# Second weights by neighbouring rows, first weights by every fourth column, in a recurrence followed by a gated MLP

## The chip, the cores and the metric

The kernel runs on one core of one Trainium2 chip. The metric is the time of one execution on the device, in microseconds. The core has five engines that run their own instruction streams: PE (TensorE: matrix products), DVE (VectorE), ACT (ScalarE), POOL (GpSimd) and SP (SyncE, which here only issues transfers). PEld stands for the loads of PE's stationary operand, which are instructions of their own. Transfers are carried by 16 DMA engines that all issuing queues share.

## The reference

The inputs are `q`, `k`, `v` and `alpha` of shape batch 4, heads 8, steps 768, head size 48, and two weight matrices. A recurrence runs over the steps of each head, and its outputs, 3072 tokens of 384 numbers, go through an MLP whose activation is `h * cos(h)`.

```python
for t in range(S):                                   # S = 768
    state = alpha[:, :, t, :, None] * state + np.einsum('bhd,bhe->bhde', k[:, :, t], v[:, :, t])
    y[:, :, t] = np.einsum('bhd,bhde->bhe', q[:, :, t], state)
...
x = y.transpose(0, 2, 1, 3).reshape(B * S, H * D)    # 3072 x 384
h = x @ w_in                                         # w_in: 384 x 2048
g = h * np.cos(h)
return g @ w_out                                     # w_out: 2048 x 384
```

The order in which the 2048 hidden columns are numbered does not matter to the result, as long as a column of `w_in` and the row of `w_out` with the same number meet in the second product.

## The kernel before

The work is cut into 12 blocks J of 256 tokens (three to a batch entry). For each block the recurrence is computed in chunks: logarithms of alpha and their running sums (`ln`, `cums0`, `cums`), exponentials (`icp`, `exps`), scaled keys and queries (`scale_k`, `scale_q`), transposes (`trans`), scores and mask, the states (`outer`, `add_state`, `decay_state`), and the transposed output (`yT`), which is evicted to `xT[J]` with 384 rows in three groups of 128 partitions and 256 token columns. Both `cums0` and `cums` end with small products in line 182: a load of 128x128 stationary numbers and a matrix product with 2 moving columns.

The MLP follows for the same block. `mlp1(J, u)` (line 390) makes one of four groups u of 512 hidden columns: `FW` = 4 tiles of 128 columns, each of `KT` = 3 accumulated products, 12 in all, with a 128x128 piece of `w1` as the stationary operand and 256 columns of `xT` as the moving one. `cosine` (ACT, line 396) and `gate` (DVE, line 401) turn the four tiles into `gsb[J]`. `mlp2` (line 419) multiplies with 16 tiles of `w2`: there `gsb` is the stationary operand and the 384 columns of `w2` move. Over the kernel there are 576 products of line 390.

Both weight matrices lie in SBUF for the whole run, in bfloat16; DRAM holds them in float32. `w1` is `[128, 3, 2048]`: partition p of group kk holds row 128 kk + p of `w_in`. `w2` is `[128, 16, 384]`. Each comes in four transfers of 384 KB (as written) that POOL issues, `load_w1(u)` (line 126) and `load_w2(u)` (line 132). They convert on the way and travel in POOL's own DMA queue, one after the other. The inputs of a block (`load`, line 110) are issued by SP, with runs of 384 bytes.

The order of the instructions on each engine is written out by hand: `PLAN` gives every step of every block a number, and the steps are emitted in that order. Where a transfer depends on nothing it is sent early; only the load of `a` for block 2 waits, until the products of `yT(1)` are done (`GATES`), and what SP issues after it stands behind it. Products of zeros (`idle`, line 445) fill some gaps of PE at the start.

Of the kernel before, what the change touches and what calls it, by code (L numbers as in the profile page):

```python
# [16 lines left out]
def kernel(  # L17
# [10 lines left out]
    nc = tc.nc  # L28
    B, H, S, D = q.shape
    DM, DF = moe_w_in.shape  # L30
    C = 128
# [8 lines left out]
    FW = 4  # L40
# [53 lines left out]
    w1 = consts.tile([C, KT, DF], BF, tag="w1", name="w1")  # L94
# [3 lines left out]
    xT, gsb = {}, {}  # L98
# [24 lines left out]
    WQ = FW * C  # L123
# [7 lines left out]
    def load_w2(u):  # L131
        nc.gpsimd.dma_start(
            out=w2[:, FW * u : FW * (u + 1)],
            in_=moe_w_out[u * WQ : (u + 1) * WQ, :].rearrange("(a p) d -> p a d", p=C),
        )

    act_now = [None]
# [245 lines left out]
    h_ps, c_sb, o_ps, o_sb = {}, {}, {}, {}  # L383

    def mlp1(J, u):
        h_ps[J, u] = ps.tile([C, FW, T2], FP, tag="h", name="h_ps", bufs=3)
        for f in range(FW):
            ft = u * FW + f
            for kk in range(KT):
                nc.tensor.matmul(h_ps[J, u][:, f, :], w1[:, kk, ft * C : (ft + 1) * C], xT[J][:, kk, :],  # L390
                                 start=(kk == 0), stop=(kk == KT - 1))

    def cosine(J, u):
# [47 lines left out]
    def idle(n):  # L441
# [6 lines left out]
    mults = {"DVE": nc.vector, "POOL": nc.gpsimd}  # L448
    steps = {
        "load": lambda J, nm: load(nm, J), "w1": load_w1, "w2": load_w2,  # L450
        "mula": mul_a, "ln": ln, "cums0": cums0, "cums": cums, "sub": sub, "icp": icp, "exps": exps, "eb": session,
        "sk": lambda J, e, eng="POOL": scale_k(J, e, mults[eng]), "sq": lambda J, e, eng="POOL": scale_q(J, e, mults[eng]),
        "castv": cast_v, "vst": stack_v, "vpe": stack_v_pe,
        "vev": lambda J, eng="DVE": evict_vs(J, copies[eng]), "decay": decay, "trans": trans,
        "evT": lambda J, c, eng="DVE": evict_T(J, c, copies[eng]), "scores": scores, "mask": mask, "outer": outer,
        "add": add_state, "state": decay_state, "yT": yT, "evy": lambda J, c, eng="ACT": evict_y(J, c, copies[eng]),
        "m1": mlp1, "sin": cosine, "gate": gate, "m2": mlp2, "evo": lambda J, c, eng="ACT": evict_o(J, c, copies[eng]),
        "out": store, "idle": idle,
    }
# [114 lines left out]
```

## Time and profile before

| | |
|---|---|
| time, median of 3 runs | 186.45 us (185.67 to 188.55) |
| the profiled execution | 185.78 us, span 184.0 us |
| granted TensorE clock | 0.999 |
| PE busy | 173.0 us, 94% of the span |
| PEld / DVE / ACT / POOL busy | 68% / 73% / 68% / 45% |
| moved by DMA | 29.47 MB in 60137 packets |

The span runs from the first instruction to the last; the execution takes 1.78 us more than that. Busy time of an engine is the time that its recorded instructions cover. The records of matrix products overlap, since a product starts before the one ahead of it has left the array, so a mean duration (273 ns in line 390) is not the time that one costs: that is the distance from one start to the next.

### The profile page before, as it was taken

The numbers are of one execution on the slowest core, as the hardware profiler recorded it, in microseconds if no ns is written. First come the engines' busy times: TensorE is split into PE (matmuls) and PEld (weight loads), VectorE is DVE, ScalarE is ACT, GpSimd is POOL, SyncE is SP. The second block draws the span as 40 slices with busy tenths as digits, with TensorE's granted clock in tenths as the row PEclk, the third lists the DMA queues.
The fourth block names the chain that finished last, engine by engine and source line by source line (L and its number), as shares of the span: only waits on it lengthen the run. The fifth ranks groups of instructions, "written<-read, shape, count | busy, mean of one in ns | idle before, by whom it ended". The sixth has DMA issues, their size and how long they took to land.

```text
span 184.0 us, 5742 instructions
## 1 busy us (share of the span) xinstructions
PE 173.0 (94%) x2457; PEld 125.5 (68%) x2458; DVE 134.5 (73%) x182; ACT 124.9 (68%) x157; POOL 83.5 (45%) x116
## 2 busy tenths in 40 slices
PE   7989579979999999999999999999899999999993
PEld 2445458646687776876787777876687677776672
DVE  7069777669999899799969898879587674734520
ACT  3745457789879999895978989869774517435201
POOL 5388550079883484939686093903901110000000
PEclk9999999999999999999999999999999999999999
DMA  6999999999999979963996579003420121010312
GB/s 146 261 248 224 216 202 206 262 256 257 261 213 262 304 170 278 260 164 85 278 289 154 140 215 245 18 6 88 143 71 4 41 88 51 0 43 4 127 44 86
DMA packets 60137, 29.47 MB, mean 160 GB/s; under 512 B 51024, under 2 KB 60112, under 8 KB 60112
## 3 DMA queue, kind: packets, MB, share of 16 engines
q1 hardware_dynamic: 56256, 25.86, 57.9%
q0 software_dynamic: 3712, 3.15, 10.6%
q8 instruction: 19, 0.31, 0.8%
q10 hardware_dynamic: 144, 0.10, 0.2%
q14 instruction: 6, 0.05, 0.1%
HBM read 25.17 MB, written 4.72 MB: 162 GB/s over the span
## 4 chain that ended last, share of the span: by engine, by line
PE 68%; DMA 11%; issue 7%; SPq 6%; POOL 5%; ACT 1%; DVE 1%; POOLq 0%; DVEq 0%
PE h_ps L390 28%; PE o_ps L419 26%; DMA v<-in_v_dram 6%; SPq L110 4%; PE y_ps L370 4%; DMA k<-in_k_dram 4%; PE A_ps L303 2%; PE T_ps L288 2%; PE U_ps L321 2%; SPq L246 2%; PE o_last L419 1%; DMA vs<-vp 1%; POOL un L343 1%; POOL a L154 1%; PE cums L168 1%
## 5 line engine op out<-in xcount | busy, mean ns | idle before, releaser
L401 DVE TENSOR_TENSOR gsb<-h_ps,c_sb 128x1024 bf16<-128x1024 f32 x48 | 58.4, 1222 | 20.0 <-ACT c_sb L396 18.8
L396 ACT ACTIVATE c_sb<-h_ps,halfpi 128x1024 bf16<-128x1024 f32 x48 | 53.4, 1114 | 28.5 <-PE h_ps L390 28.4
L390 PE MATMUL h_ps<-xT,w 128*128 128x256 bf16 x576 | 67.5, 273 | 0.7 <-DMA w<-in_moe_w_in_dram 0.5
L419 PE MATMUL o_ps<-w,gsb 128*128 128x384 bf16 x368 | 66.7, 326 | 0.0
L390 PEld LDWEIGHTS <-w 128*128 128x128 bf16 x576 | 55.4, 98 | 9.7 <-DMA w<-in_moe_w_in_dram 0.8
L419 PEld LDWEIGHTS <-gsb 128*128 128x128 bf16 x400 | 37.0, 98 | 20.8
L343 POOL TENSOR_TENSOR un<-us,c 128x384 bf16<-128x384 f32 x20 | 16.7, 836 | 33.1 <-DVE us L335 26.0
L309 DVE TENSOR_TENSOR A_sb<-A_ps,msk 128x1024 bf16<-128x1024 f32 x24 | 29.1, 1220 | 3.6 <-PE A_ps L303 3.4
L233 POOL TENSOR_TENSOR kh<-k,icp 128x384 bf16<-128x384 f32 x19 | 19.5, 1032 | 10.2 <-ACT lna L146 5.3
L237 POOL TENSOR_TENSOR qh<-q,cp 128x384 bf16<-128x384 f32 x19 | 18.8, 999 | 6.1 <-ACT cp L219 4.2
L154 POOL TENSOR_TENSOR a<-a 128x384 f32<-128x384 f32 x9 | 9.0, 997 | 11.8 <-DMA a<-in_alpha_dram 11.8
L240 POOL CAST vp<-v 128x768 bf16<-128x768 f32 x12 | 10.1, 853 | 6.4 <-DMA v<-in_v_dram 6.0
L146 ACT ACTIVATE lna<-a 128x768 bf16<-128x768 f32 x12 | 10.1, 842 | 4.1 <-DMA a<-in_alpha_dram 2.4
L141 ACT ACT_TABLE_LOAD x9 | 11.5, 1283 | 0.9 <-PEq L558 0.7
L294 DVE COPY qkT<-T_ps 128x1024 bf16<-128x1024 bf16 x17 | 11.4, 682 | 0.8 <-PE T_ps L288 0.8
L396 ACT ACT_TABLE_LOAD x9 | 11.5, 1283 | 0.2
L431 ACT COPY o_sb<-o_ps 128x384 f32<-128x384 f32 x10 | 4.8, 478 | 9.6 <-PE o_ps L419 9.6
L431 DVE COPY o_sb<-o_ps 128x384 f32<-128x384 f32 x13 | 7.2, 554 | 4.3 <-PE o_ps L419 4.2
L445 PE MATMUL idle_ps<-zeros 128*128 128x512 bf16 x28 | 9.0, 469 | 1.2 <-DVE halfpi L77 1.2
L379 DVE CAST xT<-y_ps 128x384 bf16<-128x384 f32 x14 | 7.7, 584 | 3.1 <-PE y_ps L370 2.9
L335 DVE TENSOR_TENSOR us<-U_ps,un 128x384 f32<-128x384 f32 x16 | 8.8, 551 | 1.3 <-PE U_ps L321 1.2
L303 PE MATMUL A_ps<-qkT 48*128 48x128 bf16 x192 | 8.7, 217 | 0.6 <-DVE qkT L294 0.5
(68 smaller groups left out, 149.2 us busy)
## 6 DMA issues: line engine op xcount, KB each, us to landing
a<-in_alpha_dram SPq DMA_DIRECT2D x12, 384.0 KB, 6.0
v<-in_v_dram SPq DMA_DIRECT2D x12, 384.0 KB, 6.1
k<-in_k_dram SPq DMA_DIRECT2D x12, 384.0 KB, 6.0
q<-in_q_dram SPq DMA_DIRECT2D x12, 384.0 KB, 6.2
out_dram<-o_sb SPq DMA_DIRECT2D x23, 192.0 KB, 2.3
vs<-vp SPq DMA_DIRECT2D x36, 64.0 KB, 2.8
w<-in_moe_w_in_dram POOLq DMA_DIRECT2D x4, 384.0 KB, 8.7
w<-in_moe_w_out_dram POOLq DMA_DIRECT2D x4, 384.0 KB, 10.7
```

The costliest lines, as they stand in the source:

```text
L141: nc.scalar.preload_act_table_set("natural_log_exp_and_others")
L233: eng.tensor_tensor(out=kh_t[J % NQ][:, e, :, 0:D], in0=kqv["k", J][:, :, e], in1=icp_, op=ALU.mult)
L237: eng.tensor_tensor(out=qh_t[J % NQ][:, e, :, 0:D], in0=kqv["q", J][:, :, e], in1=cp, op=ALU.mult)
L294: ins = copy(out=qkT_sb[J][:, c], in_=T_ps[J][:, c].rearrange("r n e s -> r n (e s)"))
L303: last = nc.tensor.matmul(A_ps[J, c][:, a, p, :], qkT[r, c, NP + p, :], qkT[r, c, p, :], start=True, stop=True)
L309: nc.vector.tensor_tensor(out=A_sb[J][:, c].rearrange("s a p t -> s (a p) t"), in0=A_ps.pop((J, c)).rearrange("s a p t -> s (a p) t"), in1 ...
L343: nc.gpsimd.tensor_tensor(out=u, in0=U_sum.pop(n), in1=c2_sb[J][:, :, c].unsqueeze(3).to_broadcast([C, NP, 2, D]), op=ALU.mult)
L390: nc.tensor.matmul(h_ps[J, u][:, f, :], w1[:, kk, ft * C : (ft + 1) * C], xT[J][:, kk, :], start=(kk == 0), stop=(kk == KT - 1))
L396: nc.scalar.activation(out=c_sb[J, u], in_=h_ps[J, u], func=AF.Sin, bias=halfpi, scale=1.0)
L401: nc.vector.tensor_tensor(out=gsb[J][:, u * FW : (u + 1) * FW], in0=h_ps.pop((J, u)), in1=c_sb.pop((J, u)), op=ALU.mult)
L419: nc.tensor.matmul(o[:, 0 : cols.stop - cols.start], gsb[J][:, ft, c * C : (c + 1) * C], w2[:, ft, cols], start=(done == 1 and ft == fts[0 ...
L431: copy(out=t, in_=o_ps.pop((J, c))[0][:, 0:DM])
```

## The change

Row f of the 512 rows of a transfer of `w_out` used to go to partition f mod 128, tile f div 128. Now it goes to partition f div 4, tile f mod 4: four neighbouring rows, 4 x 1536 bytes in DRAM, come to one partition, where they lie one behind the other. The transfer's shape goes from 128x4x384 to 128x1536. To match it, the hidden columns that `mlp1` puts into tile f are those with the number f mod 4, so the stationary operand is read from `w1` with a step of four columns, 128 numbers out of 512, where it was 128 numbers side by side. The loads of `w1`, all the products of line 419 and the order of the instructions on every engine stay as they were.

```diff
     def load_w2(u):
         nc.gpsimd.dma_start(
             out=w2[:, FW * u : FW * (u + 1)],
-            in_=moe_w_out[u * WQ : (u + 1) * WQ, :].rearrange("(a p) d -> p a d", p=C),
+            in_=moe_w_out[u * WQ : (u + 1) * WQ, :].rearrange("(p a) d -> p a d", p=C),
         )
...
     def mlp1(J, u):
         h_ps[J, u] = ps.tile([C, FW, T2], FP, tag="h", name="h_ps", bufs=3)
         for f in range(FW):
-            ft = u * FW + f
             for kk in range(KT):
-                nc.tensor.matmul(h_ps[J, u][:, f, :], w1[:, kk, ft * C : (ft + 1) * C], xT[J][:, kk, :],
+                cols = w1[:, kk, u * WQ : (u + 1) * WQ].rearrange("p (n a) -> p n a", a=FW)
+                nc.tensor.matmul(h_ps[J, u][:, f, :], cols[:, :, f], xT[J][:, kk, :],
                                  start=(kk == 0), stop=(kk == KT - 1))
```

## The prediction

> **What bounds the kernel now.** I read the page first: the span, the engines, the chain that ended last, and the two groups that the change can touch on PE.
>
> ```profile
> span 184.0 us, 5742 instructions
> PE 173.0 (94%) x2457; PEld 125.5 (68%) x2458; DVE 134.5 (73%) x182; ACT 124.9 (68%) x157; POOL 83.5 (45%) x116
> DMA  6999999999999979963996579003420121010312
> ...
> PE 68%; DMA 11%; issue 7%; SPq 6%; POOL 5%; ACT 1%; DVE 1%; POOLq 0%; DVEq 0%
> ...
> L390 PE MATMUL h_ps<-xT,w 128*128 128x256 bf16 x576 | 67.5, 273 | 0.7 <-DMA w<-in_moe_w_in_dram 0.5
> L390 PEld LDWEIGHTS <-w 128*128 128x128 bf16 x576 | 55.4, 98 | 9.7 <-DMA w<-in_moe_w_in_dram 0.8
> ```
>
> PE is 68% of the chain, and line 390 with its stationary loads is the largest user of it. The DMA row is at nine tenths for the first fifteen slices, so there are two stages. The chain in order of time and a table by stage show where they meet.
>
> ```profile
> 8.70 10.94 DMA v<-in_v_dram
> ...
> 25.60 10.75 issue
> ...
> 37.63 6.54 DMA k<-in_k_dram
> ...
> 51.36 0.62 PE A_ps L303 x16
> 51.98 5.35 PE h_ps L390 x48
> ...
> 74.66 5.24 PE h_ps L390 x48
> ...
> 173.00 2.60 PE o_ps L419 x16
> ...
> 180.88 0.36 DVE o_half L427
> ```
>
> ```profile
> core 0: us, PE busy (x) PEld busy (x) DVE busy (x) ACT busy (x) POOL busy (x), PEclk, DMA share, GB/s
> 0.00:51.00 51.00, 44.08 (x634) 28.45 (x635) 36.37 (x69) 33.77 (x47) 29.38 (x50) 1.00 1.15 231
> 51.00:181.00 130.00, 128.91 (x1825) 97.10 (x1823) 97.93 (x114) 91.11 (x111) 54.15 (x66) 1.00 0.53 133
> ```
>
> Until 51.36 us the chain runs mostly through transfers and their issue; the 10.75 us called issue is a wait of POOL for a transfer, as the list of waits shows below. The 16 DMA engines are fully in use then (a share above 1 means that packets overlap). From there to 180.9 us it is PE without a break, 128.91 us busy of 130, at a full clock. So an edit has to be priced twice: in the first stage by what it does to the transfers, in the second by what it does to the distance between two products.
>
> **The change, part 1: the step of four in the stationary loads.** The instructions on PE are the same in number and order; 576 loads of line 390 read every fourth column. What matters is whether a load still ends within the time of the product ahead of it. The record of a load lasts 98 ns, but that is not what it occupies. Line 182 shows it: full 128x128 loads, each followed by a product with only 2 columns.
>
> ```profile
> L182 PEld LDWEIGHTS <-lna x60: 95/96/99, 6.3 to 117.3; 128*128 128x128 bf16 x60
> ...
> L182 PE MATMUL cums_h<-inchunk,lna x24: 163/163/167, 6.5 to 37.1; 128*128 128x2 bf16 x24
> ```
>
> ```profile
> 17.32 1.47 PE L390 MATMUL h_ps<-xT,w 128*128 128x256 bf16 x12 [0.23 <-DVE xT L379]
> ...
> 36.96 0.34 PE L182 MATMUL cums_h<-inchunk,lna 128*128 128x2 bf16 x8
> ```
>
> Eight such pairs take 0.34 us; taking off one product's own record (163 ns) leaves 0.177 us for seven distances, 25 ns for a load with its product. So a contiguous load occupies at most 25 ns. In line 390 the distance is (1.47 - 0.273) / 11 = 109 ns, and 5.24 / 48 = 109 ns in the chain: 256 moving columns set it. The load has 109 - 25 = 84 ns to spare, which is the cover of this edit. A strided load costs nothing until it occupies 4.4 times what it does now.
>
> The trace before has no stationary load with a step, so its price is bounded from both sides. From below, it stays 25 ns and costs 0; nothing in the edit can make the product shorter, which excludes a gain here. From above, the 128 numbers now spread over 4 times the bytes of a partition. If the load cost rises with the bytes passed over, it is 4 x 25 = 100 ns, still inside 109, and the cost is 0. If it rises twice as steeply, 8 x 25 = 200 ns, each distance grows by 91 ns; 576 x 91 ns = 52 us. I take 0, because the nearest estimate, four times, is still covered, and keep 0 to +52 us. That cover is thin at its upper end (9 ns), and it would be gone in any line with a shorter product.
>
> The Trainium skill has a rule that could speak against the change: "Advanced Engine Details and Errata", Memory Cachelines, says that SBUF is read in lines of 16 bytes, that an access needs about two hits on a line to hide its latency, and that fewer are penalised. Columns four apart in bfloat16 are 8 bytes apart, exactly two to a line, so by that rule the cost is 0 too, at the last step before a penalty. "TensorE: Matmul & The Clock Gate", LDWEIGHTS, gives the load as columns divided by 1.2 per ns, 107 ns for 128; the trace disagrees for contiguous loads (25 ns in line 182), and should the strided one fall to that figure, the sum would still be 0 since 107 is below 109.
>
> **Part 2: the second weights' runs.** Four loads of 384 KB change from runs of 1536 bytes to runs of 6144 bytes in DRAM. They are issued by POOL in 0.8 us each, and this issue time is the same for the loads of `w1` (804 ns) with 384 runs as for these with 512 (806 ns), so I take no change of it.
>
> ```profile
> L132 POOL DMA_DIRECT2D w<-in_moe_w_out_dram x4: 782/806/806, 10.5 to 23.9; - x4
> ...
> DMA to landing us min/median/max: 9.0/10.7/11.9
> ```
>
> ```profile
> L126 POOL DMA_DIRECT2D w<-in_moe_w_in_dram x4: 775/804/927, 8.6 to 16.4; - x4
> ```
>
> ```profile
> 6.00:10.00 4.00, 3.72 (x33) 1.96 (x32) 0.56 (x1) 3.68 (x9) 2.33 (x4) 1.00 1.27 261
> 13.00:14.00 1.00, 1.00 (x19) 0.54 (x14) 0.97 (x2) 0.05 (x1) 1.00 (x3) 1.00 1.24 207
> 26.00:28.00 2.00, 1.51 (x15) 1.12 (x13) 1.15 (x2) 1.11 (x1) 0.00 (x0) 1.00 1.31 203
> ```
>
> The last column is the rate as written. I read 13 to 14 us as a load of `w1` (issued first, at 8.6 us; runs of 2048 bytes, 1024 written) and 26 to 28 us as mostly `w2` (768 written). One run on one of 16 engines then takes 16 x 1024 / 207 = 79 ns and 16 x 768 / 203 = 60.5 ns. The difference is 0.073 ns a byte, which leaves 4.6 ns a run that does not depend on its length. Joining four runs saves about 14 ns; 512 joined runs over 16 engines, 32 x 14 ns = 0.45 us out of the 7.75 us (4 x 393 KB at 203 GB/s) that these loads need. Read as an upper bound, half of the 7.75 us goes, 3.9 us; as a lower bound, nothing. I take 0.5 us, by the row it comes from.
>
> Where does it go? These loads move between 10.5 us and some 36 us (issue at 23.9 plus at most 11.9), in the stage where the DMA engines are full, so what they give up goes to the inputs. The wait that ends last there is POOL's for `a`:
>
> ```profile
> POOL a L154 <- DMA a<-in_alpha_dram: 11.8, 2, 10.8
> ```
>
> It ends 0.5 us sooner; next the chain waits for `k` (37.63 us plus 6.54), whose transfers move up with it. No wait on the second weights stands in the list, so their earlier landing releases nothing on its own.
>
> **The sum.** 0 for the loads, -0.5 us for the transfers: span 183.5 us, and with the 1.78 us around it 185.3 us against the profiled 185.78. The median shown, 186.45, is 0.67 us above that execution; the difference that I forecast is smaller than that.
>
> **The rivals.**
>
> A, slower: the strided load no longer fits under its product. It decides from a load of 109 ns on, and passes 2% at 109 + 3.7 us / 576 = 115 ns. For it: no such load is in the trace and the fourfold estimate leaves 9 ns only. Against it: 84 ns of cover. Prices: five times (125 ns) 576 x 16 ns = 9.2 us, 194.5; four times plus one contiguous load (125 to 145 ns) up to 20.7 us, 206; eight times 52 us, 238. I also put here a product slowed by its neighbour's wider read, which looks the same in the sum.
>
> B, slower by order: a run of 6144 bytes holds an engine four times as long as one of 1536, so inputs that share the engines wait longer. The load of `v` for block 1 in the chain (10.94 us) moves beside the first load of `w2`. If all of that load goes ahead of it, 393 KB / 203 GB/s = 1.9 us; twice, at the gate's loads too, 3.9 us and 189.7. Against it: the engines stay full, so what waits at one moment is served at the next. The Trainium skill, "DMA: Bandwidth & Descriptors", Queues, rings and completion order, says that an engine alternates between queues packet by packet, which would favour the longer runs; no row here counts the turns.
>
> C, faster by over 2%: the loads of `w2` lose half of their 7.75 us, and the first stage all of it: -3.9 us, 181.9. Against it: runs a third longer (2048 against 1536 bytes) move at 207 against 203 GB/s only.
>
> D, the runs are cut again on the way and nothing changes: 185.8.
>
> **How the numbers follow.** A measurement of this kernel can tell about 2% from no change, 3.7 us. Chances: the forecast 0.44, D 0.04, A 0.36, B 0.06, C 0.10. Faster by over 2% is C, 0.10; within 2% the forecast and D, 0.48; slower A and B, 0.42. The likeliest case has 183.9 to 187.5 as its own range. The range given reaches down to 183.0 and up to 206 (a load of 145 ns); outside lie most of C and the third of A that is dearer.
>
> **What would show it.** Right: the distance of line 390 in the dense stage stays 109 ns (48 products in 5.2 us), the record of its loads may grow but no idle time of PE appears; `w2` moves above 203 GB/s; line 419 stays at 2.60 us for 16 products; the dense stage begins about 50.9 us. Wrong by A: twelve products of line 390 take over 1.4 us in the chain, DVE and ACT idle more for `h_ps`, and the stage after 51 us grows by 480 times the excess.
>
> ```profile
> 51.00:181.00 130.00, 56.18 (x480) 46.36 (x480) 1.00 0.53 133
> ```
>
> Wrong by B: the load of `v` in the chain takes over 12 us and the dense stage begins after 53 us. Wrong by C: it begins before 48 us.

## The result, and the profile after

The changed kernel takes 193.7 us (median of 4 runs, 193.22 to 196.23) against 186.28 us for the one before in the same runs. The medians lie 7.4 us apart, and the ratio is 1.0423, 95% interval 1.0397 to 1.0449. The kernel is slower, inside the range given but in the other direction than the likeliest case. The ratio is that of the fast executions alone; the profiled one, at 196.23 us, is a slow one, whose excess comes at a wait between 131 and 139 us, so the readings in time below come from the part ahead of it.

The page of the changed kernel, in the lines that answer to those shown of before:

```profile
span 194.5 us, 5742 instructions
PE 175.7 (90%) x2458; PEld 133.1 (68%) x2458; DVE 134.2 (69%) x182; ACT 124.6 (64%) x157; POOL 82.4 (42%) x116
PEclk9999559999999999999999999999789999999998
DMA  6999990899999989995999097304330022010222
...
L390 PE MATMUL h_ps<-xT,w 128*128 128x256 bf16 x576 | 69.8, 278 | 9.3 <-DMA w<-in_moe_w_in_dram 8.9
L390 PEld LDWEIGHTS <-w 128*128 128x128 bf16 x576 | 63.0, 115 | 13.4 <-issue 9.8
```

The loads of line 390 are recorded at 115 ns instead of 98, and this is not the loss, as e1 below shows. What stands out is the idle time ahead of the products of that line: 9.3 us, of which 8.9 for transfers of the first weights, where it was 0.7. Two slices (19 to 29 us) show half the clock, and the slice behind them shows no traffic. (The 7 and the 8 further on in the clock's row come with the wait after 131 us.) The instructions of PE in order of time say where the wait sits:

```profile
16.85 0.40 PE L288 MATMUL T_ps<-ident_bf,qh 64*128 64x64 bf16 x16
21.74 0.38 PE L390 MATMUL h_ps<-xT,w 128*128 128x256 bf16 x1 [4.49 <-DMA w<-in_moe_w_in_dram]
26.50 2.51 PE L390 MATMUL h_ps<-xT,w 128*128 128x256 bf16 x11 [4.38 <-DMA w<-in_moe_w_in_dram]
```

Before, the first twelve products of line 390 began at 17.32 us, behind the same transposes. Now the first waits until 21.74 us and the second until 26.50 us, each for a transfer of the first weights; then the clock is halved (eleven products in 2.51 us). PE's work on the MLP begins 9.2 us later, and the chain carries that on to the dense stage, the stage in which PE works without a break:

```profile
16.57 9.79 DMA w<-in_moe_w_in_dram
26.36 0.14 issue
26.50 2.51 PE h_ps L390 x11
...
58.70 0.55 PE A_ps L303 x16
59.26 5.37 PE h_ps L390 x48
...
81.98 5.25 PE h_ps L390 x48
...
135.25 4.04 DMA vs<-vp
```

The dense stage starts at 58.70 us, not at 51.36: 7.3 us later. In it 48 products take 5.25 us, 109 ns each, as before.

What the held product waits for stands in the program as built, where every instruction lists its waits. `DMASW0`, 2, 3 and 4 are the four transfers of `w1`, in the order in which POOL issues them, and `DVE` is the eviction of `xT`:

```
before  first load of line 390, J = 0   waits DVE, DMASW0
        later groups                    wait DMASW2; DMASW3; DMASW4, each ahead of its own columns
after   first load of line 390, J = 0   waits DVE, DMASW2, DMASW0
        second load of line 390         waits DMASW4, DMASW3
```

In this program, a read side by side was tied to the transfer that writes those columns, and a read with a step to every transfer that writes the tile. The first strided product of block 0 needs the columns of `DMASW0` only, which were there when the kernel before started it at 17.32 us. It is now held until the second of the four transfers has landed (21.74 us), and the second product, which reads the same quarter of `w1`, until the last has (26.50 us). These waits together are the cause proposed by theory W, called the hold from here on. Rival L says that the strided loads cost, rival R that the long runs of the second weights hold up other transfers.

### The profile page after: what moved, and what is told of

It is laid out like the page before. It is cut to its first block, busy times and chain, and to the rows that moved or that the text cites. A ratio compares the mean times of both kernels' runs of the same rounds, so it can differ in the third digit from the quotient of the medians.

```text
span 194.5 us, 5742 instructions
## 1 busy us (share of the span) xinstructions
PE 175.7 (90%) x2458; PEld 133.1 (68%) x2458; DVE 134.2 (69%) x182; ACT 124.6 (64%) x157; POOL 82.4 (42%) x116
## 4 chain that ended last, share of the span: by engine, by line
PE 69%; DMA 10%; issue 7%; SPq 4%; POOL 4%; DVE 4%; POOLq 0%
PE h_ps L390 28%; PE o_ps L419 27%; DMA w<-in_moe_w_in_dram 5%; PE y_ps L370 5%; DMA k<-in_k_dram 3%; PE A_ps L303 3%; SPq L110 3%; PE T_ps L288 2%; DVE A_sb L309 2%; DMA vs<-vp 2%; SPq L246 2%; PE U_ps L321 2%; PE o_last L419 1%; POOL kh L233 1%; POOL un L343 1%
## 5 line engine op out<-in xcount | busy, mean ns | idle before, releaser
L390 PE MATMUL h_ps<-xT,w 128*128 128x256 bf16 x576 | 69.8, 278 | 9.3 <-DMA w<-in_moe_w_in_dram 8.9
L390 PEld LDWEIGHTS <-w 128*128 128x128 bf16 x576 | 63.0, 115 | 13.4 <-issue 9.8
L370 PE MATMUL y_ps<-A_sb,vs 128*32 128x128 bf16 x384 | 8.1, 226 | 2.4 <-DMA vs<-vp 2.4
```

Of the source, the lines that this page charges most:

```text
L370: last = nc.tensor.matmul(y_ps[J][32 * g : 32 * g + 32, c, i * C : (i + 1) * C], l, r, start=(c, g) not in begun, stop=(c, g, i) not in ou ...
L390: nc.tensor.matmul(h_ps[J, u][:, f, :], cols[:, :, f], xT[J][:, kk, :], start=(kk == 0), stop=(kk == KT - 1))
```

## The experiments

**e1, the change with the first weights in four tiles.** Each strided read then touches a tile that one transfer writes; the program waits as before (`DMASW0`, 2, 3, 4 ahead of their own columns).

```diff
-    w1 = consts.tile([C, KT, DF], BF, tag="w1", name="w1")
+    w1 = [consts.tile([C, KT, FW * C], BF, tag=f"w1_{u}", name=f"w1_{u}") for u in range(NU)]
...
-            out=w1[:, :, u * WQ : (u + 1) * WQ],
+            out=w1[u],
...
-                cols = w1[:, kk, u * WQ : (u + 1) * WQ].rearrange("p (n a) -> p n a", a=FW)
+                cols = w1[u][:, kk, :].rearrange("p (n a) -> p n a", a=FW)
```

> The change kept whole, but the first weights lie in four tiles, one for each transfer, so a strided read waits for its own transfer only. Theory W (the first strided product waits for all four transfers of the first weights, and that hold costs the time): about 185.5 us, ratio 0.994 to 1.000, the first products of line 390 start near 17 us, the load of a for block 2 is issued near 25 us. Rival L (the strided loads themselves cost): 193 us, ratio 1.04, with the loads still recorded at 113 ns. Rival R (the long runs of the second weights delay the other transfers): 193 us too.

Measured: 184.92 us, ratio 0.9958 (0.9927 to 0.9989). The whole loss is gone, with the strided loads and the long runs still in place. The products begin at 17.37 us and the dense stage at 50.15 us; the loads are recorded at 113 ns:

```profile
17.37 1.47 PE L390 MATMUL h_ps<-xT,w 128*128 128x256 bf16 x12 [0.23 <-ACT xT L379]
```

```profile
50.15 0.55 PE A_ps L303 x16
```

```profile
L390 PEld LDWEIGHTS <-w x576: 110/113/151, 17.3 to 172.6; 128*128 128x128 bf16 x192
L390 PE MATMUL h_ps<-xT,w x576: 269/273/418, 17.4 to 172.7; 128*128 128x256 bf16 x192
```

This version takes 0.4% less than the kernel before; the interval ends just short of 1, so this small gain is shown only weakly. Against this version the hold alone can be read: with the same loads and runs, the products begin 9.1 us later in the changed kernel (26.50 against 17.37) and the dense stage 8.6 us later (58.70 against 50.15).

**e2, the kernel before with the wait alone.**

```diff
+    w1_dma = {}
...
-        nc.gpsimd.dma_start(
+        w1_dma[u] = nc.gpsimd.dma_start(
...
-                nc.tensor.matmul(h_ps[J, u][:, f, :], ...
+                ins = nc.tensor.matmul(h_ps[J, u][:, f, :], ...
+                for d in list(w1_dma):
+                    tc.add_manual_dep(ins.ins, w1_dma.pop(d).ins.name, ...)
```

> The kernel before, contiguous reads and short runs, with one thing added: the first product of line 390 (here line 392) waits for all four transfers of the first weights. Theory W: 193 us, ratio 1.035 to 1.045; PE idle about 9 us before that product, clock halved in that stage, no traffic for some us around 30 us. Rivals L and R: 186 us, ratio within 0.5% of 1, since neither strided loads nor long runs are there.

Measured: 195.44 us, ratio 1.0493 (1.0442 to 1.0544), just above the interval that I had given as far as 1.045. The page has the marks of the changed kernel, with no strided load and no long run in it:

```profile
PEclk9999555799999999999999999999999999999999
DMA  6999990699998998895599547801440022010222
```

```profile
PE h_ps L392 <- DMA w<-in_moe_w_in_dram: 9.7, 1, 9.7
```

```profile
26.81 2.72 PE h_ps L392 x12
...
60.47 0.55 PE A_ps L305 x16
```

The dense stage starts 9.1 us later than before, and the span is 9.1 us longer (193.1 against 184.0). So the wait is enough by itself: it brings the whole loss without anything that L or R needs.

**e3, the long runs alone.** The diff is the first hunk of the change only.

> Only the second weights' long runs; the first weights are read side by side as before, so columns and rows of the two products no longer belong together and the output is another one. Theory W: 185.8 us, ratio 0.994 to 1.000, issue of these transfers 0.59 us instead of 0.81. Rival R: 193 us, ratio 1.04. Rival L: 186 us.

Measured: 184.72 us, ratio 0.9931 (0.9902 to 0.9959). The long runs gain 0.7%. The ratio lies just below the 0.994 to 1.000 that I had given, and R wanted a loss of 4%. In the chain, POOL's wait for `a` ends at 35.21 us (25.10 plus 10.11), 1.1 us sooner than before, and the dense stage starts at 50.11 us, 1.25 us sooner:

```profile
25.10 10.11 issue
...
50.11 0.55 PE A_ps L303 x16
```

Their marks on the page: fewer packets in POOL's queue (the same row of before first) and a shorter issue.

```profile
q0 software_dynamic: 3712, 3.15, 10.6%
```

```profile
q0 software_dynamic: 2176, 3.15, 9.5%
```

```profile
L132 POOL DMA_DIRECT2D w<-in_moe_w_out_dram x4: 583/592/604, 10.6 to 23.5; - x4
```

**e5, the step alone**, the second hunk only, with `w1` in one tile.

> Only the reads four columns apart, first weights in one tile as in the change, second weights in the old short runs (columns and rows of the two products no longer belong together, so the output is another one). Theory W: the hold alone, as in the kernel before with the added wait: ratio 1.045 to 1.055, 195 us, a little above the whole change, because the 0.7% of the long runs is missing. A rival in which hold and runs are not additive: 1.03 or below.

Measured: 195.27 us, ratio 1.0509 (1.0468 to 1.055), as e2 within the intervals. With e3 and the whole change this adds up: 1.0509 x 0.9931 = 1.0436 against 1.0423 measured.

**e8, a control:** the kernel before with four tiles for the first weights.

> The kernel before with the first weights in four tiles, reads side by side and short runs. A control: 185.6 us, ratio 0.998 to 1.002, so what the split version of the change gained comes from the runs, not from the tiles.

Measured: 185.53 us, ratio 0.9989 (0.9972 to 1.0006). The tiles by themselves do nothing that can be measured, so e1 has its gain from the runs, which gain as much without them in e3.

**e4, what a strided load occupies.** Behind the last tile, five groups of 32 products with two moving columns; the line is repeated with a step of 1, 2, 4, 8 and 16 (lines 450 to 458).

```diff
+        for i in range(32):
+            nc.tensor.matmul(t[:, 4:6], w1[:, 0, 0:512:4], inchunk, start=True, stop=True)
```

> The kernel before with 160 small products (2 moving columns) behind the last tile, 32 each with stationary columns 1, 2, 4, 8 and 16 apart. They measure what a load occupies. Theory W needs it to be far under 109 ns at step 4: I expect distances of 25 ns at steps 1 and 2, 40 ns at step 4 (25 plus the 15 ns by which the record of a load grew, 98 to 113 ns), and 40 to 60 ns at 8 and 16. Rival L needs 109 ns or more at step 4.

The timeline of PE at the end of that run (start, duration of the whole group):

```profile
180.29 0.94 PE L450 MATMUL probe_ps<-inchunk,w 128*128 128x2 bf16 x32
181.09 0.94 PE L452 MATMUL probe_ps<-inchunk,w 128*128 128x2 bf16 x32
181.90 1.21 PE L454 MATMUL probe_ps<-inchunk,w 128*128 128x2 bf16 x32
182.96 2.07 PE L456 MATMUL probe_ps<-inchunk,w 128*128 128x2 bf16 x32
184.90 2.11 PE L458 MATMUL probe_ps<-inchunk,w 128*128 128x2 bf16 x32
```

Less the record of one product (163, 163, 172, 198 and 200 ns) and divided by 31, a load with its product occupies 25 ns at steps 1 and 2, 33 ns at step 4, 60 at step 8 and 62 at step 16. I had 40 for step 4. Rival L needed 109. One caution: the granted clock is 1.00 up to 185.0 us and 0.5 from there on, so nearly all of the step-16 group ran at half the clock; its first two distances, still at the full clock, are 61 and 62 ns too. This run was executed once (189.77 us with the added products), and its time is not used.

Two more runs, e6 and e7, ask why a hold of 9 us is not absorbed by a stage that is bound by transfers. **e6, the gate earlier:**

```diff
-    GATES, AFTER = {("a", 2): ("yT", 1)}, {}
+    GATES, AFTER = {("a", 2): ("yT", 0)}, {}
```

> The change with the load of a for block 2 released by yT(0) instead of yT(1), which PE reaches before the held product. Theory G (the hold costs time because the inputs of the later blocks are released behind it, so the DMA engines stand idle for 5 us): no idle stretch of the DMA engines around 30 us; the inputs share the engines with the weights, so the hold ends later, near 29 to 31 us, but the dense stage starts earlier than 58.7 us, near 54 to 56; 189 to 191 us. Rival P (the hold costs PE's own time, 9 us of products that have to be made up): no gain, 193 us or more.

Measured: 193.9 us, ratio 1.0446 (1.0412 to 1.0479), no gain. Theory G falls. The load of `a` is issued at 16.58 us instead of 34.70 (the first line is the changed kernel's, the second this run's) and the engines have no empty slice around 30 us any more. The hold ends at 27.29 us, not at 29 to 31 as I had expected, yet the dense stage starts at 59.50 us:

```profile
34.70 0.99 SPq L110 DMA_DIRECT2D a<-in_alpha_dram  x2
```

```profile
16.58 3.68 SPq L110 DMA_DIRECT2D a<-in_alpha_dram  x2
```

```profile
DMA  6999999995959969395899357701530022010212
```

```profile
27.29 2.50 PE h_ps L390 x11
...
59.50 0.55 PE A_ps L303 x16
```

From the end of the hold to the dense stage it is 59.50 - 27.29 = 32.2 us here and 58.70 - 26.50 = 32.2 us in the changed kernel, whether the inputs come early or late, and PE is busy for 30.4 us of it in both. Rival P holds: the products that stand behind the held one have to be made up. The tables by stage show PE with little room for it, the kernel before first, then the changed one:

```profile
17.00:26.00 9.00, 6.23 (x132) 4.85 (x125) 7.10 (x11) 5.08 (x6) 6.00 (x9) 1.00 1.23 214
...
34.00:51.40 17.40, 16.10 (x253) 10.18 (x253) 13.57 (x19) 14.94 (x24) 12.33 (x15) 1.00 1.12 257
```

```profile
17.00:26.00 9.00, 0.63 (x19) 0.24 (x11) 2.05 (x4) 1.62 (x2) 3.33 (x6) 0.63 1.21 226
...
30.00:34.00 4.00, 2.53 (x60) 2.25 (x63) 4.00 (x5) 1.34 (x3) 1.37 (x2) 1.00 0.00 0
34.00:58.70 24.70, 24.52 (x372) 18.42 (x362) 20.01 (x26) 21.98 (x31) 13.30 (x16) 1.00 1.06 235
```

PE did 0.63 us of work in the 9 us from 17 to 26 us (before, 6.23), and from 34 us on it is busy for 24.52 of 24.70 us. That the DMA engines carry nothing from 30 to 34 us is a consequence, not the price: without that gap e6 is no faster.

**e7, zeros in front of the held product**, so that PE stays busy.

```diff
-    IDLE = [(45, 10), (155, 2), (345, 9), (375, 1), (435, 4), (485, 3)]
+    IDLE = [(45, 10), (155, 2), (345, 9), (375, 1), (435, 4), (485, 3), (555, 42)]
```

> The change with 42 products of zeros (about 9 us) in front of the held product, so PE is not idle while it waits and its clock stays full. Theory: the halved clock in the 10 us from 19 to 30 us costs the products behind the hold 1.3 us (eleven of line 390 took 2.51 us instead of 1.25): 191.5 to 192.5 us, dense stage about 57.5 us. Rival: the clock does not matter beside the transfers, 193 us.

Measured: 193.52 us, ratio 1.0422 (1.0368 to 1.0476), where I had expected 191.5 to 192.5. In the profile the clock stays full and the products behind the hold go at full speed:

```profile
17.04 9.17 PE idle_ps L445 x42
...
26.46 1.36 PE h_ps L390 x11
...
57.31 0.55 PE A_ps L303 x16
```

The dense stage starts 1.4 us earlier than in the changed kernel, of which 1.15 us is those eleven products (2.51 against 1.36). The measured time does not show it: the interval of the ratio is 1 us wide to either side. So the clock's share of the loss is about 1 us at most, and whether it reaches the end of the kernel stays open.

## Why the prediction was wrong

The step that failed is the first sentence of its part 1: "The instructions on PE are the same in number and order", and from there that the only question was whether a load ends under its product. The instructions are the same, their waits are not. The edit tied the first two strided products to three transfers whose columns they do not read. The prediction put this at nothing without a reason; I did not ask which transfers a strided read is tied to. The wait alone costs 9.1 us (e2). None of the rivals had it: A put the slow side on the load, B on the inputs.

Point by point:

- The cover of the loads: right. The distance stayed 109 ns and the record grew to 113 ns. The estimate of four times 25 ns was too high; it is 33 ns, and even steps of 8 and 16 (60 and 62 ns) are below 109.
- The rule on lines of 16 bytes from the Trainium skill ("Advanced Engine Details and Errata", Memory Cachelines): by it two hits on a line are enough to hide the latency. In e4 they cost 33 against 25 ns, so little, but not nothing, and one hit on a line (steps 8 and 16) costs 60 and 62 ns. The trace agrees that the large step lies between two hits and one.
- The long runs: right in sign and in path (the wait for `a`), mis-sized. The term was -0.5 us; e3 measured -0.7%, 1.3 us of 185.6. POOL's queue took 10.6% of 184.0 us before and 9.5% of 182.8 us in e3, 19.5 against 17.4 us of all 16 engines: 2.1 us, where two rows of nearby lengths had given 0.45. With 1536 packets fewer that is 22 ns a packet (16 x 2.1 us over 1536), not the 4.6 ns of the prediction. Its working divided by the rate alone and left out that packets overlapped in those rows (shares of 1.24 and 1.31): 79 x 1.24 = 98 ns and 60.5 x 1.31 = 79 ns leave 23 ns a packet. And the issue, taken as unchanged, fell from 806 to 592 ns.
- "In the first stage by what it does to the transfers": too narrow. The stage was read as bound by transfers because the chain ran through them, and e3 shows that the long runs do shorten it. But PE was idle for only 6.9 of its 51 us before, and e6 shows that, in its fixed order, it has no room for 9 us either.
- What would show it wrong: the mark set down for B, a dense stage after 53 us, came (58.70 us), but the other half of that mark, a load of `v` of over 12 us, did not: the longest took 10.2 us, before 10.9. The chain goes through `w1`, and e3 excludes B. For the right side I had written that no idle time of PE would appear; 9.3 us did.

The sum as it should have been: the wait +9.1 us (e2 against before), the long runs -1.3 us (e3), the strided loads 0 (e1 and e3 lie within each other's intervals; their medians are 0.2 us apart): +7.8 us. The medians of the two kernels lie 7.4 us apart, and the ratio of 1.0423 gives 7.9. That the time came out inside the stated range was luck: the range reached up for slow loads, which did not come.

## What to carry to other kernels

An edit that changes only how a tile is read can change what the read waits for: compare the waits of the built program, not only its instructions. If a tile that several transfers fill piece by piece is to be read with a step, try it as several tiles, one for each transfer; here that removed the whole loss. And a stage whose chain runs through transfers may still have no room on an engine that works in a fixed order: here 8.6 of 9.1 us of the hold came through to the next stage.

## What the runs showed of the hardware that I had not expected

In e4, a load of 128 stationary columns together with a product of 2 columns occupies 25 ns at a step of 1 or 2 in bfloat16, 33 ns at 4, and about 60 ns at 8 and at 16 alike, at step 16 with the granted clock at 1.00 as at 0.5. The record of the load (97 ns at step 2, 118 at step 4, 173 at step 16 in e4) is far longer than what it occupies. The transfers that POOL issues took 806 ns each to issue with 512 runs and 592 ns with 128, while 384 runs in the other weights took 804.
